# Fewer tiles in the second copy of x, a padded bias block, and a new written-out order

## The chip, the cores and the metric

The kernel runs on one core of a Trainium2 chip. The metric is the device time of one execution in microseconds (us), the median over runs. The engines are TensorE (PE), VectorE (DVE), ScalarE (ACT), GpSimd (POOL) and SyncE (SP), which here only issues transfers.

## The reference

Two branches over x (2048 rows, 512 columns), mixed by a gate:

```python
x = A_x
g = _sigmoid((x * gate_w).sum(-1, keepdims=True))
a = irfft2(rfft2(x) * (w_r + 1j * w_i))          # spectral branch, 2048 x 512
h = einsum("bsd,df->bsf", x, w1) + b1            # dense branch, 512 -> 1792 -> 512
b = einsum("bsf,fd->bsd", h * tanh(softplus(h)), w2)
return g * a + (1 - g) * b
```

Inputs and output are bfloat16.

## The kernel before

x is held as 16 tiles of 128 rows, tile t being the rows that are t modulo 16. The dense branch works in four chunks of four tiles. For each chunk c, 14 groups mm1_c_ft multiply w1 by the transposed x (xT) into PSUM; mish_c_ft on ACT adds b1 (b1f) and applies the activation; mm2_t_part multiplies by w2. In chunk 0 the first four groups are cut into halves by columns and by contraction (mm1a0_ft, mm1a1_ft, mm1b0_ft, mm1b1_ft).

The spectral branch: ts and td on DVE form sums and differences of x; s1 (PE), e2 (eviction), a10 and a11 (PE), eg (ACT), e1p and e1m (DVE) make the first transforms; r1w stores the result to a scratch in DRAM, r1r loads it turned round; s2 (PE), wm and wz (DVE, POOL), s2i (PE), e4, r2w and r2r do the same for the second axis; s1i, e5, a1i, gc, sap, sam, sbp, sbm go back. gdot, gpow, gcol and omg make the gate.

xT comes in two ways. Tiles 0 to 7 are transposed on PE (tr, L475) into PSUM and evicted (evx). Tiles 8 to 15 are loaded a second time in 16 small copies (ld_xq, rows of 256 bytes) into a buffer X4, which lies in the third part of act, and transposed from there in blocks by DVE (xt, L483). b1 is loaded by POOL's queue (ld_b1) as 14 rows into braw, transposed by PE (tr_small, L488) and evicted by DVE (ev_small, L490). At the start PE runs matmuls on constants (warm, L419) while nothing has been loaded.

The order is written out by hand. Every operation is a task with a number in the order in which the code adds it; the string ORDER lists the tasks by two digits in base 62, with a letter where a task may run on several engines and a digit for each PSUM bank. Each engine runs its own tasks in that order, and waits on semaphores for what a task reads, or overwrites:

```python
for t in order[ename]:
    ...
            eobj.wait_ge(sem_, val)
    ins = t.fn(eobj)
```

So a task that waits holds back everything behind it on its engine, loads included, as an engine's queue also issues its transfers. A task that writes a tile waits for the tile's last writer:

```python
for w in writes:
    _add(self.last_w.get(w))
    for rd in self.readers.get(w, ()):
        _add(rd)
```

Of the kernel before, what the change touches and what calls it, by code (L numbers as in the profile page):

```python
# [7 lines left out]
BF = mybir.dt.bfloat16  # L8
# [5 lines left out]
NT = 16  # L14
# [143 lines left out]
class _Graph:  # L158
# [89 lines left out]
DIGITS = "0123456789ABCDEFGHIJKLMNOPQRSTUVWXYZabcdefghijklmnopqrstuvwxyz"  # L248
ENGINE = {"p": "pe", "a": "act", "v": "dve", "g": "pool", "s": "sp"}
ORDER = (  # L250
    "000M1Wv02010P0Q0R0S0U1Xv0W0X0Y0Z04005060708090A0B0C0D0E0F0G0H0I0J0K0L030q0N0O1E70a1Fv0V0b0r1G30c0T111I61Hv0d6u"
    "70s1K0121Zv6z3701Jv1g41U61Yv1p11Lv0e1ia6v1hv1V71721rv745751qa1j40t731l1bv761av776w1s23A6x1k4791781u0f1t2131mv2"
    "051nv1wv1og0g0h0i6y0j7B31dv7A21a1vv7D11M72267C2302837F21cv7E1Nv242I529a26v7H71xv1ev2A325v7G2B12Ja2C7J01fv7I2K5"
    "2Q20u0v7L42u2M2L62Dv2Ra7N72Ev2a12v2Ov2S57M2w2Nv2T37K7P07O2Fg6p727g0k0l0m0n0o0p2x1y2U2ba2k56q142Vv2y6r1O2156s2l"
    "a2c12Pg2Wv2e2n52m32z1Pv6t2Xg2d67R42fv302gv1z2G2H0w2o0x7f12qv2hg2rg2Y162pv2Z2i2j2s1S7S2t17310y1A0z7g1018191R7Q3"
    "27h21Q3K1T7i33343536377j6387k393B3F3C7l07m1B3G3D3E3L7n77o7p17q7r07t47v77s7x37u7w7z08127y835848573H3I3J82808J18"
    "68K8L38N28P68M8O8R38S8T78Q8V23O33Wv3P53R8U8W1C3Q3Xv3S3T3Yg8X18Z23Zg3bv3U8Y3V8b78a8c8d18f33av3e8g3M8e7T73j33l3k"
    "13m3n3qv3cg8h53rv7U3o7W03N1D3uv3p3dg3vv8i7X3sg3y3f17Ya3tg3xg7Vv3ga4353wg4Av7Z77a3ha454Bv4Dg44046473z340a3i41a7"
    "c24Cg4849424I7d4Fv4Ev4Hg4Gg7bv4N54O34Vv4P4Q4R8j07ev877884Uv8A68B4S4Zv4T4Yv4c8k4J04Kv89a4Wg4Xg4La4bg4ag8D74d14f"
    "v8x58Cv8E4ea8Fv8z38y8G59129348H92957948Iv976908l08m8nv96989978o34M4g4h4i9A4l14mv4t25105974j52v4ua5H65Aa5P54n14"  # L260
    "o5X44v25305Iv5B74p4w4q5C4sg4rg4x8p4y5E5f64zg545gv5Qa5Ya5D50g565J15R59B2558qa5K9iv4k5n49C9D79jv5S5U5Fg5h25v65L5"
    "oa5M5wa9F35T9G5Gg5Z49H66336B55i9I64v57g5a58g9J19L05p36569lv9mv5Og5j5Wg5b5Vg9K9M6Ca5k5c9E8r15Ng9ov5x25y9pv6J46R"
    "0605lg5q5s6D75mg9k6Ka5eg6Sa5z5r5dg6661g8s8ta6E6F6Z46av9sv6h09rv62g5ug8u55tg679N29O6G8v8wa686Ag6L39n6T46U6W6M9P"
    "16O9uv6b29vv6c9Q69g9xv6ia6j06V9S69q9t6e6Hg9Ra6d6k9w6N6Ig9yv9T9V56fv9W6Xg6l6m6Yg9Z49z6gv9c26nv6Qg6Pg9Ua9X9YA0vA"
    "1v9f5A26ov9d9a9e9b9g9h"
)
NBF = 14
GD_N = 8
# [8 lines left out]
DENSE2 = {0: (0, 1), 1: (0, 1), 2: (0, 1, 2, 7), 3: (0, 1, 2, 7)}  # L277
LAST = ((0, 256), (256, 384), (384, 512))
NWARM = 16
NFILL = 2  # L280
PR = dict(tr=99.0, sp=95.0, mm1=88.0, mish=97.0, mm2=70.0, fin=98.0, gate=96.9, sum=98.5)


def _build(nc, A_x, A_w_r, A_w_i, B_x, B_w1, B_b1, B_w2, gate_w, out):
    cs = _build_consts()
    d_FM, d_GM, d_RT = (nc.inline_tensor(_bf16_bits(cs[n].reshape(128, -1)), name="c_" + n.lower()).bitcast(BF)
                                    for n in ("FM", "GM", "RT"))
# [3 lines left out]
    G = _Graph()  # L291
    es = ExitStack()
    with es:
        def sb(name, shape, dt):
            return es.enter_context(nc.sbuf_tensor(name, shape, dt))

        xo = sb("xo", [128, NT, 512], BF)
        xT = sb("xT", [128, 4, NT * 128], BF)
        Tg = sb("Tg", [128, 8192], BF)
        act = sb("act", [128, 3, NFT, 512], BF)  # L300
# [4 lines left out]
        rt = sb("rt", [128, 4096], BF)  # L305
# [2 lines left out]
        WT = sb("WT", [128, 2, 16, KR], BF)  # L308
        Abuf = sb("Abuf", [128, 8192], BF)
        Ybuf = sb("Ybuf", [128, 16 * 514], BF)  # L310
        braw = sb("braw", [14, 128], BF)
        b1f = sb("b1f", [128, NFT], F32)
        gdot = sb("gdot", [128, NT], F32)
        gcol = sb("gcol", [128, NT], F32)
# [1 line left out]
        ident = sb("ident", [128, 128], BF)  # L316
# [12 lines left out]
        REV = [31 - d for d in range(32)]  # L329
        REV0 = [(32 - d) % 32 for d in range(32)]  # L330
        XS = Abuf[:, 0:8192].rearrange("p (t r d) -> p t r d", t=NT, r=2)
        X4 = act[:, 2].rearrange("p f s -> p (f s)")[:, 0:4096].rearrange("p (t q d) -> p t q d", t=8, q=4)
        In2 = Abuf[:, 0:8192].rearrange("p (u g k) -> p u g k", u=8, g=4)
        T2r = Abuf[:, 0:8192].rearrange("p (b k) -> p b k", b=32)
        Yt = Ybuf[:].rearrange("p (t x) -> p t x", t=NT)
# [30 lines left out]
        def dma(name, dst, src, reads=(), writes=(), nbytes=0, deps=(), is_out=False, prio=None, queue="sp", bw=380e3, tail=1.1, nd=128, issue=0.62):  # L366
            t = G.add(name, queue, issue if issue != 0.62 or queue != "pool" else 1.0, lambda e: e.dma_start(dst, src),
                      reads=reads, writes=writes, lat=tail, deps=deps, prio=prio)
# [12 lines left out]
        def mm(n):
            return n / 2400.0 + 0.0025
# [10 lines left out]
        def pe(name, dur, fn, **kw):  # L393
            return G.add(name, "pe", dur, fn, lat=0.17, **kw)
# [7 lines left out]
        def tt(name, o, i0, i1, op, n, rate=1.0, engs=("dve",), lock=True, **kw):  # L402
# [8 lines left out]
              reads=["ones"], writes=["ident"])  # L411
# [3 lines left out]
        pw = _Ps([6])  # L415
        tw = []
        for i in range(NWARM + NFILL):
            n = 256 if i < NWARM else 128
            tw.append(pe(f"warm{i}", mm(n), lambda e, n=n: e.matmul(ps[:, pw.bank, 0:n], nc.const_aps.tensor(1.0, [128, 128], BF), nc.const_aps.tensor(1.0, [128, n], BF), start=True, stop=True),  # L419
                         alloc=pw if i == 0 else None, frees=[pw], prio=0.0, deps=tw[-1:]))  # L420

# [39 lines left out]
        dma("ld_ri", rt[:, 2048:4096], d_RT[:, 2048:4096], writes=["RI"], nbytes=128 * 4096, bw=300e3)
        WALL = [("W", i, j) for i in range(2) for j in range(9)]


        for t0, h in ((0, 0), (0, 1), (2, 0), (2, 1), (4, None), (6, None)):
            pt = _Ps(SPEC[::-1])
            hs = (0, 1) if h is None else (h,)
            c0, nc_ = 2 * hs[0], 2 * len(hs)

            def f_tr(e, t0=t0, c0=c0, nc_=nc_, pt=pt):  # L470
                ins = None
                for i in range(2):
                    for c in range(c0, c0 + nc_):
                        o = ((c - c0) * 2 + i) * 128
                        ins = e.transpose(psb[:, pt.bank, o:o + 128], xo[:, t0 + i, c::4], ident[:, :])  # L475
                return ins

            pe(f"tr{t0}" + ("" if h is None else "ab"[h]), 2 * nc_ * mm(128), f_tr, reads=[("x", t0 + i) for i in range(2)] + ["ident"], writes=[("ptr", t0, h)], alloc=pt)
            evict(f"evx{t0}" + ("" if h is None else "ab"[h]), 256 * nc_, lambda t0=t0, c0=c0, nc_=nc_: xT[:, c0:c0 + nc_, 128 * t0:128 * (t0 + 2)],
                  lambda pt=pt, nc_=nc_: psb[:, pt.bank, 0:256 * nc_].rearrange("p (c j) -> p c j", c=nc_), rate=2.0,  # L480
                  reads=[("ptr", t0, h)], writes=[("xT", t0 + i, q) for i in range(2) for q in hs], frees=[pt], engs=("dve",) if h is None else ("dve", "act"))
        for t0 in range(8, NT, 2):
            G.add(f"xt_{t0}", "dve", dve_dur(1024), lambda e, t0=t0: e.transpose(  # L483
                out=xT[:, :, 128 * t0:128 * (t0 + 2)], in_=X4[:, t0 - 8:t0 - 6, :, :].rearrange("p t q (d b) -> p b (t q) d", b=4)),
                reads=[("X4", a, q) for a in range(4) for q in range(4)] + [("act", 2, f) for f in range(t0 - 8, t0 - 6)],
                writes=[("xT", t0 + i, q) for i in range(2) for q in range(2)], lock=True, prio=PR["tr"] - 12.0 - 0.5 * t0)
        pb = _Ps(SPEC[::-1])
        pe("tr_small", 0.1, lambda e, pb=pb: e.transpose(psb[:, pb.bank, 0:14], braw[0:14, :], ident[0:14, 0:14]),  # L488
           reads=["braw", "ident"], writes=["ptb"], alloc=pb)
        G.add("ev_small", "dve", 0.2, lambda e, pb=pb: e.tensor_copy(out=b1f[:, :], in_=psb[:, pb.bank, 0:14]),  # L490
              reads=["ptb", "b1t"], writes=["b1f"], frees=[pb])
# [9 lines left out]
        for t in range(NT):  # L501
            if t % 2 == 0:
                p1 = _Ps(S1B)

                def f_s1(e, t=t, p1=p1):
                    ins = None
                    for i in range(2):
                        for q in range(4):
# [4 lines left out]
                                   writes=[("p1", t)], alloc=p1, prio=PR["sp"] + 0.4))  # L513
# [418 lines left out]
```

## Time and profile before

| | us |
|---|---|
| median of 3 runs | 129.48 (128.7 to 129.66) |
| the profiled execution | 129.57 |
| its span, first to last instruction | 127.8 |
| PE busy | 121.1 (95%) |
| DVE busy | 92.1 (72%) |
| ACT busy | 70.3 (55%) |
| POOL busy | 52.6 (41%) |

The profile is of one execution. The span is what its instructions cover; the rest of its time lies around it. A line such as L475 is a line of the kernel's code; helpers record several operations under one line (L403 is every tensor-tensor operation, L367 every transfer, L398 and L397 the evictions on ACT and DVE). Views used: the page's busy shares and its 40 slices of the span, the waits (who stood idle for whom), the timeline (start, duration, engine, line, what), the chain of waits that ended last, groups of instructions, and the transfers with their time from issue to landing.

### The profile page before, as it was taken

Reading aid. Unit: us, or ns where it says so; the run is one execution under the profiler, and the core shown is the slowest. Engines: PE = TensorE matmul, PEld = TensorE weight load, DVE = VectorE, ACT = ScalarE, POOL = GpSimd, SP = SyncE. Lnnn points to the kernel's source line nnn. Section 1 sums busy time; section 2 is a strip of 40 time slices with the busy share of each in tenths; the row PEclk is TensorE's granted clock in tenths of the full one; section 3 lists DMA queues with packets and bytes.
Section 4 is the critical chain, followed back from the end, with each engine's and each line's share of the span. In section 5 each row is a group of like instructions: output and inputs, shape, how many; then the busy total and the mean of one; then the engine's idle time right before and its main releaser. Section 6 shows DMA issues by size and latency. Waiting matters only on the chain.

```text
span 127.8 us, 2747 instructions
## 1 busy us (share of the span) xinstructions
PE 121.1 (95%) x1038; PEld 67.8 (53%) x1055; DVE 92.1 (72%) x190; ACT 70.3 (55%) x113; POOL 52.6 (41%) x82
## 2 busy tenths in 40 slices
PE   7799999999999969999999999999999999999992
PEld 5687666844444334444444444444576556454481
DVE  0769999999994089597679737020399999879853
ACT  4069999898839635416242235153299878354200
POOL 5000004110004457889685950000019979676500
DMA  3999999989878999800523008359200222022213
GB/s 85 352 395 388 286 175 177 206 235 266 255 186 224 258 374 371 341 24 5 164 63 109 0 0 229 107 146 405 105 0 5 82 85 82 0 87 82 82 42 122
DMA packets 23053, 21.10 MB, mean 165 GB/s; under 512 B 5888, under 2 KB 20096, under 8 KB 22912
## 3 DMA queue, kind: packets, MB, share of 16 engines
q1 hardware_dynamic: 22192, 20.13, 54.5%
q10 hardware_dynamic: 816, 0.79, 1.9%
q8 instruction: 8, 0.13, 0.5%
q14 instruction: 5, 0.04, 0.1%
q0 software_dynamic: 32, 0.00, 0.0%
HBM read 14.63 MB, written 6.29 MB: 164 GB/s over the span
## 4 chain that ended last, share of the span: by engine, by line
PE 79%; DMA 8%; DVE 5%; ACT 4%; issue 2%; SPq 0%; DVEq 0%
PE ps L797 36%; PE ps L767 30%; DMA Abuf<-scr 5%; DMA xo<-in_A_x_dram 3%; DVE Qb L739 3%; PE ps L534 2%; PE ps L509 2%; PE ps L717 2%; PE ps L689 2%; PE ps L638 2%; PE ps L728 2%; ACT Qb L733 1%; ACT act L782 1%; PE ps L475 1%; DVE xo L403 1%
## 5 line engine op out<-in xcount | busy, mean ns | idle before, releaser
L767 PE MATMUL ps<-xT,w_sb 128*128 128x512 bf16 (+1 forms) x230 | 52.0, 364 | 0.7 <-DVE cvec L645 0.2
L797 PE MATMUL ps<-w_sb,act 128*128 128x512 bf16 (+2 forms) x245 | 50.2, 355 | 0.7 <-issue 0.5
L782 ACT ACTIVATE act<-ps,b1f 128x512 bf16<-128x512 f32 x56 | 36.7, 689 | 24.2 <-PE ps L767 24.0
L797 PEld LDWEIGHTS ps<-w_sb,act 128*128 128x128 bf16 x252 | 23.0, 98 | 23.4 <-issue 0.6
L767 PEld LDWEIGHTS ps<-xT,w_sb 128*128 128x128 bf16 x240 | 22.2, 98 | 21.8 <-issue 0.8
L403 POOL TENSOR_TENSOR Tg<-Qb 128x256 bf16<-128x256 f32 x28 | 21.1, 785 | 23.6 <-DVE Qb L739 23.6
L403 POOL TENSOR_TENSOR Zb<-Qb 128x510 bf16<-128x510 f32 x16 | 19.9, 1267 | 3.6 <-DVE Qb L403 2.9
L403 DVE TENSOR_TENSOR Qb<-ps,WT 128x1024 f32<-128x1024 f32 x16 | 18.8, 1214 | 2.0 <-PE ps L638 2.0
L739 DVE SCALAR_TENSOR_TENSOR Qb<-ps,gcol,Qb 128x256 f32<-128x256 f32 x32 | 13.4, 472 | 1.6 <-PE ps L728 0.8
L550 POOL COPY Ybuf<-Ybuf 128x2 bf16<-128x2 bf16 x7 | 2.5, 361 | 24.0 <-DVE Ybuf L403 24.0
L750 DVE TENSOR_SCALAR xo<-ps,omg 128x512 bf16<-128x512 f32 x7 | 5.2, 745 | 9.4 <-PE ps L797 9.4
L563 DVE SCALAR_TENSOR_TENSOR Tg<-xo,Tg 128x512 bf16<-128x512 bf16 x16 | 10.9, 678 | 0.2
L403 DVE TENSOR_TENSOR Ybuf<-ps,Tg 128x512 bf16<-128x512 f32 x16 | 10.5, 683 | 0.5 <-PE ps L534 0.2
L398 ACT ACTIVATE Tg<-ps 128x1024 bf16<-128x1024 f32 (+1 forms) x8 | 7.4, 922 | 5.5 <-PE ps L509 5.3
L749 ACT ACTIVATE xo<-ps,omg 128x512 bf16<-128x512 f32 x7 | 4.8, 690 | 9.7 <-PE ps L797 9.7
L403 DVE TENSOR_TENSOR xo<-xo,Tg 128x512 bf16<-128x512 bf16 x14 | 9.9, 746 | 0.0
L398 ACT ACTIVATE Ybuf<-ps 128x1024 bf16<-128x1024 f32 x6 | 5.9, 1022 | 6.6 <-PE ps L689 6.6
L403 DVE TENSOR_TENSOR Abuf<-xo 128x1024 bf16<-128x1024 bf16 (+1 forms) x10 | 5.6, 578 | 4.8 <-DMA xo<-in_A_x_dram 4.8
L733 ACT ACTIVATE Qb<-ps,gcol 128x256 f32<-128x256 f32 x16 | 7.2, 474 | 1.2 <-PE ps L728 1.2
L568 POOL TENSOR_TENSOR gcol<-omg,gdot 128x16 f32<-128x16 f32 x1 | 2.9, 2943 | 11.2 <-DVE Tg L563 11.2
L398 ACT ACTIVATE Zb<-ps 128x512 bf16<-128x512 f32 x10 | 5.6, 597 | 1.3 <-PE ps L717 1.3
L397 DVE CAST Zb<-ps 128x512 bf16<-128x512 f32 x6 | 4.0, 685 | 1.9 <-PE ps L717 1.8
(59 smaller groups left out, 90.2 us busy)
## 6 DMA issues: line engine op xcount, KB each, us to landing
Abuf<-scr SPq DMA_DIRECT2D x8, 512.0 KB, 6.4
scr<-Ybuf SPq DMA_DIRECT2D x4, 512.0 KB, 3.3
w_sb<-in_B_w_dram SPq DMA_DIRECT2D x2, 896.0 KB, 9.9
out_dram<-xo SPq DMA_DIRECT2D x7, 256.0 KB, 2.0
xo<-in_A_x_dram SPq DMA_DIRECT2D x3, 512.0 KB, 7.0
scr<-Ybuf SPq DMA_DIRECT2D x6, 256.0 KB, 3.7
act<-in_A_x_dram SPq DMA_DIRECT2D x16, 64.0 KB, 5.9
rt<-c_rt SPq DMA_DIRECT2D x2, 512.0 KB, 8.0
```

The costliest lines, as they stand in the source:

```text
L397: fs = {"dve": ("dve", dve_dur(n, rate=rate), lambda e: e.tensor_copy(out=dst(), in_=src())), "act": ("act", act_dur(n), lambda e: e.activ ...
L398: "act": ("act", act_dur(n), lambda e: e.activation(dst(), src(), AF.Copy)),
L403: f = lambda e: e.tensor_tensor(out=o(), in0=i0(), in1=i1(), op=op)
L563: lambda e, t=t: e.scalar_tensor_tensor(out=junk, in0=xo[:, t, :], scalar=1.0, in1=gwb, op0=ALU.mult, op1=ALU.mult, accum_out=gdot[:, t:t ...
L568: G.add("gpow", "pool", 3.0, lambda e: e.tensor_tensor(out=gcol[:, :], in0=omg[:, :], in1=gdot[:, :], op=ALU.pow), reads=[("gd", t) for t ...
L733: lambda e, t=t, sl=sl, p5=p5: e.activation(gC[:, sl, :].rearrange("p (i n) -> p i n", i=2), ps[:, p5.bank, :].rearrange("p (i n) -> p i n ...
L739: lambda e, t=t, sl=sl, p5=p5, o=o, op=op: e.scalar_tensor_tensor(out=st1[:, sl, o::2, :], in0=ps[:, p5.bank, :].rearrange("p (i n) -> p i ...
L749: G.add_multi(f"bev_{t}", [("act", act_dur(512, True), lambda e: e.activation(xo[:, t, :], ps[:, pd.bank, :], AF.Copy, scale=omg[:, t:t + ...
L750: ("dve", dve_dur(512, True), lambda e: e.tensor_scalar(out=xo[:, t, :], in0=ps[:, pd.bank, :], scalar1=omg[:, t:t + 1], scalar2=None, op0 ...
L767: ins = e.matmul(ps[:, pd.bank, cols[0]:cols[1]], w1_sb[:, i, 128 * ft:128 * (ft + 1)], xT[:, i, 512 * c + cols[0]:512 * c + cols[1]], sta ...
L782: lambda e, ft=ft, pd=pd, hb=hb: e.activation(act[:, hb, ft, :], ps[:, pd.bank, :], AF.Mish, bias=b1f[:, ft:ft + 1]),
L797: ins = e.matmul(ps[:, pd.bank, cs_], act[:, hb, ft, 128 * tl:128 * (tl + 1)], w2_sb[:, ft, cs_], start=(ft == 0), stop=(ft == NFT - 1))
```

## The change

- The second copy X4 holds tiles 12 to 15 only: the 16 ld_xq copies are of 32 KB instead of 64 KB. Tiles 8 to 11 are transposed by PE: two new groups tr8 and tr10 (8 transposes each) with evictions evx8 and evx10 on DVE replace xt_8 and xt_10.
- braw has 128 rows; a DVE memset (bz) sets it to zero, ld_b1 fills the first 14 rows, tr_small transposes the whole block.
- Three idle matmuls of 256 columns follow the first 16 (warm16 to warm18), instead of two of 128.
- ORDER is new, and with it the PSUM banks and the engines of some evictions.

```diff
-NFILL = 2
+NFILL = 3
...
-        braw = sb("braw", [14, 128], BF)
+        braw = sb("braw", [128, 128], BF)
...
-        X4 = act[:, 2].rearrange("p f s -> p (f s)")[:, 0:4096].rearrange("p (t q d) -> p t q d", t=8, q=4)
+        X4 = act[:, 2].rearrange("p f s -> p (f s)")[:, 0:2048].rearrange("p (t q d) -> p t q d", t=4, q=4)
...
-            n = 256 if i < NWARM else 128
+            n = 256
...
-        dma("ld_b1", braw[:, :], B_b1.rearrange("(ft p) -> ft p", p=128), writes=["braw"], nbytes=3584, queue="pool")
+        G.add("bz", "dve", 0.2, lambda e: e.memset(braw[:, :], 0.0), writes=["braw"])
+        dma("ld_b1", braw[0:14, :], B_b1.rearrange("(ft p) -> ft p", p=128), writes=["braw"], nbytes=3584, queue="pool")
...
-                dma(f"ld_xq{a}{q}", X4[32 * a:32 * a + 32, :, q, :], xv[32 * q:32 * q + 32, 8:16, 128 * a:128 * a + 128],
-                    writes=[("X4", a, q)], nbytes=32 * 8 * 256, bw=165e3, nd=256, issue=0.5)
+                dma(f"ld_xq{a}{q}", X4[32 * a:32 * a + 32, :, q, :], xv[32 * q:32 * q + 32, 12:16, 128 * a:128 * a + 128],
+                    writes=[("X4", a, q)], nbytes=32 * 4 * 256, bw=160e3, nd=128, issue=0.5)
...
-        for t0, h in ((0, 0), (0, 1), (2, 0), (2, 1), (4, None), (6, None)):
+        for t0, h in ((0, 0), (0, 1), (2, 0), (2, 1), (4, None), (6, None), (8, None), (10, None)):
...
-        for t0 in range(8, NT, 2):
+        for t0 in range(12, NT, 2):
...
-        pe("tr_small", 0.1, lambda e, pb=pb: e.transpose(psb[:, pb.bank, 0:14], braw[0:14, :], ident[0:14, 0:14]),
+        pe("tr_small", mm(128), lambda e, pb=pb: e.transpose(psb[:, pb.bank, 0:128], braw[:, :], ident[:, :]),
```

The task numbers of ORDER, read against the order in which the code adds the tasks, give these beginnings of the engines' queues:

```
SP   before: ld_x0 ld_x2 ld_ms ld_fm ld_w1_4_0 ld_x4 ld_x8 ld_w1_8_0 ld_w1_8_1 ld_x12 ld_gm ld_xq00 ...
SP   after:  ld_xq30 ld_xq20 ld_xq10 ld_x0 ld_xq31 ld_x2 ld_xq21 ld_ms ld_fm ld_w1_4_0 ld_x4 ld_x8 ...
ACT  before: table ld_w1_0_0 ld_w1_0_1 ld_w1_4_1 e2_0b e2_2a mish_0_2 eg_0 mish_0_3 ...
ACT  after:  table ld_w1_0_0 ld_w1_0_1 evx0b evx2a e2_0b ld_w1_4_1 e2_2b mish_0_2 eg_0 eg_2 ...
DVE  before: ts0 td0 evx0a evx0b td2 evx2a ts2 evx2b e2_0a ev_small e2_2b td4 ts4 e1p_0 ...
DVE  after:  td0 bz ts0 evx0a ts2 evx2b td2 ev_small e2_0a e2_2a ts4 td4 e1p_0 ...
POOL before: ones ebz ident ld_b1 ...
POOL after:  ebz ones ident ld_b1 ...
PE   before: warm0-17 tr0a tr0b tr2a mm1a0_1 tr2b mm1a0_2 mm1a1_2 s1_0 tr_small s1_2 mm1a1_1 mm1b0_2
             mm1b1_2 mm1a0_3 mm1a1_3 a10_0 mm1b0_3 mm1b1_3 mm1b0_1 a10_2 mm1b1_1 a11_0 mm1_0_4 ...
PE   after:  warm0-15 tr0a warm16-18 tr0b mm1a0_2 mm1a0_3 tr2a tr2b s1_0 mm1a1_3 mm1a1_2 tr_small mm1b0_3
             s1_2 mm1a0_1 mm1b0_2 mm1b1_2 mm1a1_1 mm1b0_1 a10_0 a11_0 mm1b1_3 a10_2 mm1_0_4 ...
```

Later on PE: tr8 and tr10 stand behind mm1_0_13, one mm1 group fewer stands ahead of s2_0 (six of chunk 2 instead of seven), and s1i_0 follows mm2_8_1 instead of mm2_9_0. On SP, all loads of the filter (ld_W) stand ahead of most of the stores r1w, and of the stores r1w14a and r1w14b only ld_rf is left between them and r1r0; before, seven loads were. On both sides 57 transfers stand ahead of r1r0.

More of the change, by code (lines that the diff above doesn't have):

```diff
@@ L250 @@
 ORDER = (
[L251 to L265, printed above, removed]
+    "0o0k02030g0N000430p0506071bv08090A0B0C0W0D0E0F0G0H0I0J011G20Q0l0R0S0K0L0T0V0Y0M1av0Z0a0b1Hv0O1I67310P7840X1cv1"
@@ new lines @@
+    "K01Ja1M51Nv1dv1La1k213790c741ma1Y71Z7A1lv1t51uv0U0h6y00q1ev1fv0s75766z701n31o70m1va0d0e777B1w21p7D61y7C7E1O524"
+    "1711x31qv1rv7F47H70i721Pv2C51hv25a0t1gv7G7I2M17J01zv20v2Dv0r0n21v2631jv0f2742Na7L7282Av2U229v1Q67K0u2E01iv3E7N"
+    "57M2Va1Rv2G2O72F32P47P12Bg2Iv2Hv7O1sv2Q2Sv7Q2Rv2e57R72W32o12X40v0w0x2Jg2y2fa2g62z2pa0y7T0147V52Y300z1S21U12av1"
+    "011122Zv2bg7U157W2h3222Tg6t531320j232K6u7S6v2q72i2kv2jv2s7j07k2r416176w181Tv6x2tv192lv1A1B2L2uv2vv2c2d2m2n2w2x"
+    "331Vv34351W1C363O3P3J3K3L7l77n3371D1E7m3Q7p53R7r77t27o1F7q7s7v57x67z07u7y3M7w388113N3982801X8323A8485486871897"
@@ new lines @@
+    "883B3C3D3F8N38O8P28R08T58Q8S8U8V18A8X03S43bv3U3av3dg3T63ev3G8W3cg3fv8Y3V3W8Z23X3Y8b08c8d38a8e8f58h48g8j38k3n63"
+    "p3hg3o13q3uv3r3s3gg3vv3Z8l53H3I3i7X03zv8m8i3yv7Y7Za7a37b3j44713ka3wg7d0493t423la3xg4Fv40g7e7ca4864Ev41g4317g54"
+    "A4B4Iv7fa44a4Gg7h45a4Jv4Hg3m4R14Zv4C4Kg4S64D7ia4T4M4U4V4W4Yv4Lg8n44bg4X8B38C8o8E58Da4N04Oa4Pa4cv4ag4dv4eg8F4g8"
+    "H68Gv4fg4h24ja9174iv929319509748I94969908K79A469B2988L4Q4k4l8Ja9C9D28p48q8Ma9E4m4n4p74x15565D24ya56a8rv5Ev8s34"
+    "qa4z15L75051524r04s4t54g5F64u5Ma5G5T45b55I5725ca53g5Uv8t585H4vg5j75ka8ua5A9F05V55W595N44wg4o5O9H69I9G5Kg5Y5r19"
@@ L266 @@
+    "nv5d75e5P8v35Q5Bg5z467660a68a9mv5Cg5sv6F09J25Jg5X5g9pv5l56Ga9K9qv5Zg616625ag5f645Rg8w6915Sg5m5n9L79tv5o5hg9o9r"
+    "5t4636N09sv8xa5u5w9M5v9N25ig9O6Oa5pg9P39u6V76d28y56A6Wa5qg6ev6H76X49Q6B9vv6Y9wv6I5xg9R29S6P366g6C65g6l66J5yg6E"
+    "g6Q6K6S6ma6f08z9zv9yv6Z6R6Dg9x6Lg6a9T6A06g90a6h6n76Mg6o6i9U9W39X9Z09a9d2A1vA2v6Ug6Tg6p9Vv6qA36kv6bg9YaA4v6jv6s"
+    "v6cgA5vA69b6rg9g69c9e9f9h9i9j49k9l"
 )
@@ L457, in _build @@
             dma(f"ld_Wz{i}", WT[1:32:2, i, 0, :], Vm[:, 63, :], writes=[("W", i, 8)], nbytes=16 * 514, bw=110e3, nd=16)
-        dma("ld_rf", rt[:, 0:2048], d_RT[:, 0:2048], writes=["RF"], nbytes=128 * 4096, bw=300e3)
+        dma("ld_rf", rt[:, 0:2048], d_RT[:, 0:2048], writes=["RF"], nbytes=128 * 4096, bw=170e3)
         for h in range(2):
@@ L481, in _build @@
                   reads=[("ptr", t0, h)], writes=[("xT", t0 + i, q) for i in range(2) for q in hs], frees=[pt], engs=("dve",) if h is None else ("dve", "act"))
-        for t0 in range(8, NT, 2):
+        for t0 in range(12, NT, 2):
             G.add(f"xt_{t0}", "dve", dve_dur(1024), lambda e, t0=t0: e.transpose(
-                out=xT[:, :, 128 * t0:128 * (t0 + 2)], in_=X4[:, t0 - 8:t0 - 6, :, :].rearrange("p t q (d b) -> p b (t q) d", b=4)),
-                reads=[("X4", a, q) for a in range(4) for q in range(4)] + [("act", 2, f) for f in range(t0 - 8, t0 - 6)],
+                out=xT[:, :, 128 * t0:128 * (t0 + 2)], in_=X4[:, t0 - 12:t0 - 10, :, :].rearrange("p t q (d b) -> p b (t q) d", b=4)),
+                reads=[("X4", a, q) for a in range(4) for q in range(4)] + [("act", 2, f) for f in range(t0 - 12, t0 - 10)],
                 writes=[("xT", t0 + i, q) for i in range(2) for q in range(2)], lock=True, prio=PR["tr"] - 12.0 - 0.5 * t0)
         pb = _Ps(SPEC[::-1])
-        pe("tr_small", 0.1, lambda e, pb=pb: e.transpose(psb[:, pb.bank, 0:14], braw[0:14, :], ident[0:14, 0:14]),
+        pe("tr_small", mm(128), lambda e, pb=pb: e.transpose(psb[:, pb.bank, 0:128], braw[:, :], ident[:, :]),
            reads=["braw", "ident"], writes=["ptb"], alloc=pb)
```

## The prediction

> **What bounds the kernel now.** I read the page's busy rows first, then the waits of TensorE (PE), then the start and the one hole in PE's timeline.
>
> ```profile
> span 127.8 us, 2747 instructions
> PE 121.1 (95%) x1038; PEld 67.8 (53%) x1055; DVE 92.1 (72%) x190; ACT 70.3 (55%) x113; POOL 52.6 (41%) x82
> PE   7799999999999969999999999999999999999992
> ...
> PE ps L638 <- DMA Abuf<-scr: 1.0, 1, 1.0
> PE ps L419 <- PEq L917: 0.8, 1, 0.8
> PE ps L475 <- DMA xo<-in_A_x_dram: 0.8, 1, 0.8
> PE ps L797 <- issue: 0.5, 3, 0.2
> PE ps L717 <- DVE Qb L739: 0.2, 1, 0.2
> PE ps L767 <- DVE cvec L645: 0.2, 1, 0.2
> PE ps L767 <- issue: 0.2, 1, 0.2
> ```
>
> PE is busy 95% of the span, and all its waits together are 3.7 us, of which 0.8 is the wait for the program's start and 0.8 the wait for the second block of x. From then on it has about 2.1 us of waiting, of which 1.04 is one hole in front of s2_0. So PE's own queue sets the end: whatever holds PE up near the start reaches the end, unless it is taken out of that hole; and an operation added to PE costs its length.
>
> The rows of the start, from the timeline:
>
> ```profile
> 0.80 0.86 SPq L367 DMA_DIRECT2D xo<-in_A_x_dram  x2
> 1.07 1.50 ACTq L367 DMA_DIRECT2D w_sb<-in_B_w_dram  x3
> 1.47 0.78 POOL L367 DMA_DIRECT2D braw<-in_B_b_dram  x1
> 3.15 1.16 SPq L367 DMA_DIRECT2D xo<-in_A_x_dram  x2
> 4.05 0.76 DVE L403 TENSOR_TENSOR Abuf<-xo 128x512 bf16<-128x512 bf16 x2 [4.05 <-DMA xo<-in_A_x_dram]
> 4.07 0.63 PE L475 MATMUL ps<-ident,xo 128*128 128x128 bf16 x8
> 5.49 0.41 PE L475 MATMUL ps<-ident,xo 128*128 128x128 bf16 x4 [0.78 <-DMA xo<-in_A_x_dram]
> 7.36 0.18 PE L488 MATMUL ps<-ident,braw 14*128 14x14 bf16 x1
> 10.78 0.81 PE L767 MATMUL ps<-xT,w_sb 128*128 128x512 bf16 x3
> ```
>
> The reader is to see four moments. ld_x0 is issued at 0.80 and lands at 4.05, 3.25 us later; PE's first transposes start then. ld_x2 is issued behind it (1.24) and lands at 5.49. The transpose of b1 (tr_small) runs at 7.36 without a wait, since its load was issued at 1.47. The first whole group of 512 columns, mm1_0_4, runs at 10.78.
>
> **The change, part by part: the start.** Three xq copies now stand ahead of ld_x0 on SP. Five issues fill 0.80 to 3.15, 0.47 us each, so ld_x0 is issued at 0.80 + 1.41 = 2.21 and, by the same 3.25, lands at 5.46. From both sides: the six xq issues of the row below take 0.51 each, which gives 5.6; on the low side, the two halves of w1 on ACT's queue get the engines first and are further along when x0 begins.
>
> ```profile
> 20.15 3.07 SPq L367 DMA_DIRECT2D act<-in_A_x_dram  x6
> ...
> 2.00:3.00 1.00, 1.00 (x7) 0.69 (x6) 0.00 (x0) 0.28 (x2) 0.38 (x2) 1.00 0.79 219
> 3.00:4.00 1.00, 1.00 (x8) 0.77 (x7) 0.00 (x0) 0.00 (x0) 0.00 (x0) 1.00 0.80 245
> 4.00:5.00 1.00, 0.70 (x12) 0.54 (x9) 0.95 (x3) 0.00 (x0) 0.00 (x0) 1.00 1.05 389
> ```
>
> x0's 256 KB at 389 GB/s instead of 245 (last column) would come 0.4 earlier, 5.05. I take 5.3, the middle; PE's start moves by 1.25. PE has nothing that covers it: the warm-up matmuls end at 4.06.
>
> Then the load of b1. The new memset bz writes braw on DVE, and ld_b1 writes the same tile, so POOL's ld_b1 waits for bz. bz stands on DVE behind td0, and td0 waits for x0. So a load that was issued at 1.47 is now issued after x0 has landed: 5.3, td0 0.38 (two in 0.76), bz 0.2 (the nearest row is POOL's memset of a 128x128 tile), 5.9. What it takes from there:
>
> ```profile
> 0.79 0.20 POOL L408 MEMSET ident<- 128x128 bf16 x1 [0.29 <-POOLq L917]
> ...
> DMA to landing us min/median/max: 5.3/5.3/5.3
> ...
> out_dram<-xo SPq DMA_DIRECT2D x2, 32.0 KB, 1.5
> ```
>
> The view of the tile braw has 5.3 us from the issue to the landing of 3.5 KB. It is the only load on POOL's queue, and I take it: 5.9 + 5.3 = 11.2. Low bound: POOL's 0.78 plus the 1.5 of the quickest small transfer of SP, 2.3, which gives 8.2. The Trainium skill ("DMA: Bandwidth & Descriptors", section "Anatomy of one DMA — SWDGE (gpsimd) path") puts a load from GpSimd at about 2.0 us plus its bytes at 436 GB/s; by that rule b1 would be there at 7.9 and the wait below would be none. The trace's 5.3 differs from it, and the measurement decides.
>
> When does PE get to tr_small? x0 5.3; tr0a, three warm-up matmuls of 256 columns (0.11 each) and tr0b, 0.8 us: 6.1. evx0a on DVE comes after td0, bz and ts0 (5.3 + 0.38 + 0.2 + 0.38 = 6.26) and takes 0.42: 6.7; two mm1 halves of 0.22: 7.15. ld_x2 is now sixth on SP, issued at 3.15, and by its old 4.24 lands at 7.4; tr2a, tr2b, s1_0 and two more halves: 0.45 + 0.45 + 0.43, 8.7. There PE waits for b1 until 11.2, some 2.5 us; ev_small, behind it on DVE, holds e2_0a and e2_2a back, and on ACT every mish waits for b1f.
>
> The shift: tr_small starts at 11.2 instead of 7.36, 3.84 later, with one half matmul (0.22) more already done: +3.6.
>
> ```profile
> 8.09 1.09 PE ps L767 x10
> ...
> 13.98 0.45 PE ps L475 x8
> ```
>
> (Ten halves in 1.09; eight transposes in 0.45, from the chain.) The padded tr_small is at most one more such transpose, 0.06: left out. Next late is ld_w1_4_1, which now stands on ACT behind evx0b, evx2a and e2_0b: e2_0b can start at 8.2 and ends at 8.8.
>
> ```profile
> w_sb<-in_B_w_dram ACTq DMA_DIRECT2D x3, 256.0 KB, 5.0
> ...
> xo<-in_A_x_dram SPq DMA_DIRECT2D x2, 256.0 KB, 3.7
> ```
>
> By the 5.0 of its queue it lands at 13.8 (by 3.7, 12.5). PE needs it for mm1_0_4, which stands 2.6 us of work behind tr_small (six halves, s1_2, three a1 groups): 13.85 by the sum above. So it is covered, by the wait for b1; without that wait it would be the one that holds PE, from 11.35 to between 12.5 and 13.8.
>
> **The transposes.** tr8 and tr10 add 16 transposes to PE: 2 x 0.45, 0.89 by the finer 0.0557 each, with nothing to hide in. On DVE two transposes are replaced by two evictions:
>
> ```profile
> L483 DVE STREAM_TRANSPOSE xT<-act 128x1024 bf16<-128x1024 bf16 x4 | 4.8, 1226 | 0.0
> L397 DVE COPY xT<-ps 128x1024 bf16<-128x1024 bf16 x2 | 1.4, 688 | 0.0
> ```
>
> That frees 1.1 us of DVE, but mm1_2_0, which reads them, stands 14 groups of four 512-column matmuls later on PE; worth nothing. If evx10 came after those 14 groups, PE would wait for it, at its whole lateness.
>
> **The hole before s2_0.** It is set by the queue of SP:
>
> ```profile
> 30.88 3.79 SPq L367 DMA_DIRECT2D scr<-Ybuf  x5
> ...
> 37.93 1.27 SPq L367 DMA_DIRECT2D WT<-in_A_w_i_dram  x2
> 39.59 0.35 SPq L367 DMA_DIRECT2D Abuf<-scr  x1
> ...
> 45.88 0.63 PE L638 MATMUL ps<-Abuf,rt 64*32 64x256 bf16 x32 [1.04 <-DMA Abuf<-scr]
> ...
> scr<-Ybuf SPq DMA_DIRECT2D x4, 128.0 KB, 2.5
> ```
>
> r1r0 is issued at 39.59, behind 57 others, and lands 6.25 later. After the change 57 still stand ahead of it, but the last stores r1w14 are now 55th and 56th instead of seven loads earlier. At the old pace the 56th is issued at 37.9, lands 2.5 later, and r1r0 goes at 40.4: data at 46.7. Half-size xq copies may make the queue 1 to 2 us faster; a late DVE could hold it, but the five stores above were issued from 30.9, so their data was ready, and 3.6 later is still before 37.9. PE came to s2_0 at 44.84; it now has one matmul group less in front (0.86), the shift and the transposes: 44.84 - 0.86 + 3.6 + 0.89 = 48.5. It no longer waits: -1.04.
>
> **The rest.** About ten evictions of the later stages change between DVE and ACT, and s1i_0 is one mm2 half group (1.5 us) nearer to s2i_3, 13.6 us of matmuls behind it instead of 15.1.
>
> ```profile
> 76.35 0.57 PE ps L689 x32
> ...
> 83.20 1.76 SPq L367 DMA_DIRECT2D Abuf<-scr  x4
> ...
> DMA to landing us min/median/max: 4.0/5.3/6.6
> ```
>
> s2i_3 ended at 76.9, so s1i_0 would come at 90.5; r2r0, issued at 83.2, lands in 4.0 to 6.6 us, by 89.8 at the latest, so there is cover. PE waits for only about 1 us in that whole part, so I count zero, with 0 to -0.8 and up to +0.8 as bounds.
>
> **Sum**, against the profiled execution (129.57 us: the span of 127.8 and 1.8 around it, which stay; the median of the runs is 129.48, the same for this purpose): +3.6 (start) + 0.89 (transposes) - 1.04 (hole) = +3.45, 133.0 us.
>
> **Rivals.**
>
> Quick b1. POOL's load takes 2.3 us instead of 5.3 (for: 3.5 KB should not need 5; against: the only row). Then ld_w1_4_1 decides: mm1_0_4 at 12.5 to 13.8 instead of 10.78, with one half not yet done, +1.9 to +3.2; plus 0.89 less 1.04; and by the r1r0 estimate PE then waits at most 0.1. Time 131.3 to 132.6.
>
> Cold clock. PE stands still some 2.5 us before tr_small, after a first stretch in which it is half idle. The matmuls of 256 columns at the start are slow: about five new ones in the microsecond from 2 to 3 (the row above counts seven with those that overlap its edges), where the later ones take 0.109. If the wait brings the slow speed back for some 2.6 us, half of it is lost, +1.3, and up to +1.8 with a second such stretch: 134.3 to 134.8. Against it: the 0.78 us hole at 4.7 left the speed as it was. The Trainium skill ("TensorE: Matmul & The Clock Gate", section "Part 1: The HAM clock gate") has the slow clock return after an idle window of about 3.4 us; by that rule 2.5 us is too short unless b1 comes a microsecond later still.
>
> Not slower: the start costs almost nothing. x0's landing is set by the slow first microseconds of the transfers (219 and 245 GB/s) and not by its issue, so it lands by 4.4, and b1 takes 2.3. PE is at tr_small near 7.8 and at mm1_0_4 near 10.5, w1_4_1 (issued at 7.9, 3.7) lands at 11.6; shift +1.0, and 0.89 - 1.04 on top, and part of the other 1 us of PE's waits taken away by the new evictions: 129.4 to 130.4. It decides only if x0 lands before 4.4 and b1 within 3 us of its issue, both. Speaks for it: half a megabyte of 256-byte rows less in the queue. Against: five issues in a row at 0.47.
>
> **How the numbers follow.** Sum as worked out (132.4 to 133.8): 0.55. Quick b1: 0.20. Cold clock: 0.12. Not slower: 0.09. Something in the later stages that I count as zero going wrong by more than 2 us: 0.04. Predicted 133.0, range 130.7 to 134.8. A measurement of this kernel tells about 1% from no change, 128.2 to 130.8: faster 0.03 (only if all waits of PE vanish too), same 0.08, slower 0.89.
>
> **What would show it.** In the profile after: DVE's first instruction at 5.0 to 5.6 instead of 4.05; POOL's DMA issue near 5.9 instead of 1.47; PE waiting 2 to 3 us for the DMA of braw ahead of the L488 transpose, which starts near 11; mm1_0_4 near 13.9; no wait at the first L638, near 48.5; 16 more L475 matmuls. Wrong if the L488 row has no wait in front of it, if the transpose starts before 9, or if PE's matmuls of 256 columns are 0.2 us apart after it.

## The result and the profile after

The changed kernel takes 137.53 us (median of 4 runs, 137.43 to 137.97) against 129.16 before in the same comparison: ratio 1.065, interval 1.060 to 1.071. It is slower, as forecast, but by 8.4 us and not by 3.5. The page of the profile after, first the busy rows and the slices of the span (PEclk is the granted clock of PE in tenths), then PE's waits:

```profile
span 136.2 us, 2791 instructions
PE 125.9 (92%) x1055; PEld 71.3 (52%) x1072; DVE 87.5 (64%) x185; ACT 75.3 (55%) x121; POOL 53.4 (39%) x80
PE   7591959999999999999999999999999999999993
PEclk9999599999999999999999999999999999999999
...
PE ps L489 <- DMA braw<-in_B_b_dram: 3.0, 1, 3.0
PE ps L768 <- ACT act L783: 1.5, 2, 1.4
PE ps L476 <- DMA xo<-in_A_x_dram: 1.5, 1, 1.5
```

All the loss is in the first six of the 40 slices; from there on PE is as full as before. (Line numbers are one higher than before, so L489 is tr_small, L476 the transposes, L510 s1, L768 mm1, L783 mish; in most variants below they are five higher again: L494, L481, L515, L773, and L424 the idle matmuls.) Rows picked from the timeline of the start, and s2_0:

```profile
2.18 0.43 SPq L367 DMA_DIRECT2D xo<-in_A_x_dram  x1
5.92 0.43 DVE L403 TENSOR_TENSOR Abuf<-xo 128x512 bf16<-128x512 bf16 x1 [5.92 <-DMA xo<-in_A_x_dram]
6.72 0.78 POOL L367 DMA_DIRECT2D braw<-in_B_b_dram  x1 [5.33 <-DVE Abuf L403]
10.22 0.37 ACTq L367 DMA_DIRECT2D w_sb<-in_B_w_dram  x1
13.65 0.29 PE L489 MATMUL ps<-ident,braw 128*128 128x128 bf16 x1 [2.99 <-DMA braw<-in_B_b_dram]
19.51 0.81 PE L768 MATMUL ps<-xT,w_sb 128*128 128x512 bf16 x3 [1.39 <-ACT act L783]
53.74 0.63 PE L639 MATMUL ps<-Abuf,rt 64*32 64x256 bf16 x32
```

The steps that the prediction named are there one by one: x0 lands at 5.92, ld_b1 is issued behind bz at 6.72, PE waits for it before tr_small, and there is no wait ahead of s2_0 (L639). What PE loses: tr_small comes at 13.65 instead of 7.36, 6.3 later; mm1_0_4 at 19.5 instead of 10.78, 8.7 later; s2_0, with one matmul group less in front of it, at 53.7 instead of 45.88, 7.9 later.

One row must not be believed as it stands. The wait of 1.39 at mm1_0_4 is put down to ACT. But mm1_0_4 reads nothing that mish writes, and its bank was not held by a mish. The row also has three of the group's four matmuls: the record of the first is missing (in the profile before too), and the weights of the group were loaded from 19.26 on, before that mish ended at 19.33:

```profile
18.65 0.68 ACT L783 ACTIVATE act<-ps,b1f 128x512 bf16<-128x512 f32 x1
19.26 0.56 PEld L768 LDWEIGHTS ps<-xT,w_sb 128*128 128x128 bf16 x4 [1.32 <-issue]
```

So mm1_0_4 began near 19.3, and PE waited some 1.2 us for it, from 18.1. The load that it does need, ld_w1_4_1, was issued on ACT at 10.22; the view of its landing, for the stretch in which it is the only issue of that tile:

```profile
L367 ACTq DMA_DIRECT2D w_sb<-in_B_w_dram x1: 374/374/374, 10.2 to 10.2; - x1
...
DMA to landing us min/median/max: 8.9/8.9/8.9
```

10.22 + 8.9 = 19.1: that load is what mm1_0_4 waited for. The experiments e1 and e6 below bear this out.

Then the clock, by stretches of one microsecond (length, PE busy, granted clock, share of the transfer engines, GB/s):

```profile
12.00:13.00 1.00, 0.00 (x0) 1.00 1.08 412
13.00:14.00 1.00, 0.35 (x3) 0.78 1.05 402
14.00:15.00 1.00, 1.00 (x10) 0.50 1.11 282
15.00:16.00 1.00, 1.00 (x8) 0.50 1.07 196
16.00:17.00 1.00, 1.00 (x7) 0.52 1.14 261
17.00:18.00 1.00, 1.00 (x16) 1.00 1.33 251
```

At the end of the wait for b1 the granted clock falls to half and stays there for 3.4 us (13.56 to 16.97 in the trace's records of the clock). The work between tr_small and mm1_0_4 took 4.5 us (13.65 to 18.1). In e4 and e7 below, which have the same order there and no slow clock, it takes 2.7 (7.49 to 10.19 and 10.80 to 13.51), so the slow clock cost 1.8.

There is an earlier slow stretch that this column does not show. The first record of the clock in this trace is of 10.14; for the time before it the view prints 1.00, but the rows are those of half speed:

```profile
8.27 1.06 PE L476 MATMUL ps<-ident,xo 128*128 128x128 bf16 x8
9.12 1.06 PE L510 MATMUL ps<-FMs,Abuf 128*128 128x128 bf16 x8
```

From the start of one row to the next, eight transposes take 0.85 us here; in the chain of before they took 0.45. From x0's landing PE needs 4.7 us to reach the wait for b1 (5.94 to 10.67); in e7, at full speed, 2.8 (8.03 to 10.80). On PE the wait for b1 covers this. But ld_w1_4_1 stands on ACT behind evictions of that work: it was issued 4.3 us after x0's landing, in e6, at full speed, 3.15 (3.93 to 7.08). What this 1.15 cost at mm1_0_4 was not tested.

### The profile page after: what moved, and what is told of

Same layout as the page of the kernel before. It is cut to its first block, busy times and chain, and to the rows that moved or that the text cites. A ratio compares the mean times of both kernels' runs of the same rounds, so it can differ in the third digit from the quotient of the medians.

```text
span 136.2 us, 2791 instructions
## 1 busy us (share of the span) xinstructions
PE 125.9 (92%) x1055; PEld 71.3 (52%) x1072; DVE 87.5 (64%) x185; ACT 75.3 (55%) x121; POOL 53.4 (39%) x80
## 4 chain that ended last, share of the span: by engine, by line
PE 86%; DMA 8%; ACT 1%; issue 1%; SPq 1%; DVE 1%
PE ps L768 36%; PE ps L798 35%; DMA braw<-in_B_b_dram 5%; DMA xo<-in_A_x_dram 3%; PE ps L729 3%; PE ps L535 3%; PE ps L718 3%; PE ps L510 3%; PE ps L690 2%; PE ps L639 1%; PE ps L476 1%; ACT act L783 1%; SPq L367 1%; DVE Abuf L403 1%; ACT Tg L542 0%
## 5 line engine op out<-in xcount | busy, mean ns | idle before, releaser
L768 PE MATMUL ps<-xT,w_sb 128*128 128x512 bf16 (+1 forms) x231 | 53.4, 374 | 2.0 <-ACT act L783 1.5
L783 ACT ACTIVATE act<-ps,b1f 128x512 bf16<-128x512 f32 x56 | 36.7, 687 | 15.1 <-PE ps L768 14.9
L768 PEld LDWEIGHTS ps<-xT,w_sb 128*128 128x128 bf16 x240 | 23.0, 102 | 22.9 <-issue 2.2
L403 POOL TENSOR_TENSOR Tg<-Qb 128x256 bf16<-128x256 f32 x29 | 22.2, 801 | 22.0 <-DVE Qb L740 22.0
L750 ACT ACTIVATE xo<-ps,omg 128x512 bf16<-128x512 f32 x11 | 7.6, 689 | 11.3 <-PE ps L798 11.3
L751 DVE TENSOR_SCALAR xo<-ps,omg 128x512 bf16<-128x512 f32 x3 | 2.2, 745 | 15.4 <-PE ps L798 15.4
L551 POOL COPY Ybuf<-Ybuf 128x2 bf16<-128x2 bf16 x4 | 0.7, 192 | 26.3 <-DVE Ybuf L403 26.3
L403 DVE TENSOR_TENSOR xo<-xo,Tg 128x512 bf16<-128x512 bf16 x14 | 10.8, 796 | 0.0
L398 ACT ACTIVATE Tg<-ps 128x1024 bf16<-128x1024 f32 (+1 forms) x7 | 6.3, 898 | 5.6 <-PE ps L510 5.5
L398 ACT ACTIVATE Zb<-ps 128x512 bf16<-128x512 f32 x12 | 6.8, 597 | 4.3 <-PE ps L718 3.8
L476 PE MATMUL ps<-ident,xo 128*128 128x128 bf16 x48 | 4.6, 249 | 1.5 <-DMA xo<-in_A_x_dram 1.5
L397 DVE COPY xT<-ps 128x1024 bf16<-128x1024 bf16 (+1 forms) x6 | 3.6, 596 | 3.3 <-PE ps L476 3.3
```

Of the source, the lines that this page charges most:

```text
L398: "act": ("act", act_dur(n), lambda e: e.activation(dst(), src(), AF.Copy)),
L403: f = lambda e: e.tensor_tensor(out=o(), in0=i0(), in1=i1(), op=op)
L750: G.add_multi(f"bev_{t}", [("act", act_dur(512, True), lambda e: e.activation(xo[:, t, :], ps[:, pd.bank, :], AF.Copy, scale=omg[:, t:t + ...
L768: ins = e.matmul(ps[:, pd.bank, cols[0]:cols[1]], w1_sb[:, i, 128 * ft:128 * (ft + 1)], xT[:, i, 512 * c + cols[0]:512 * c + cols[1]], sta ...
L783: lambda e, ft=ft, pd=pd, hb=hb: e.activation(act[:, hb, ft, :], ps[:, pd.bank, :], AF.Mish, bias=b1f[:, ft:ft + 1]),
```

## The experiments

Two theories stood at first. Theory 1: three loads that come late at the start, x0, b1 and ld_w1_4_1, cover one another in part, and the slow clock is added. The rival: the transposes and the new order of the later stages cost a part of it. All variants move tasks within their engine's queue after ORDER has been read, and nothing else, unless said:

```diff
+        for eng, name, before in (...):
+            o = order[eng]
+            t = next(t for t in o if t.name == name)
+            o.remove(t)
+            o.insert(next(i for i, u in enumerate(o) if u.name == before), t)
         self.order = order
```

**e1_bz_first**: `("dve", "bz", "td0")`, so the memset comes first and b1 is loaded at 1.5 again.

> The changed kernel with the memset bz first on DVE, ahead of td0, so that ld_b1 is issued near 1.5 instead of 6.72. Theory 1 (two late loads stand one behind the other: b1, and ld_w1_4_1, which is issued at 10.2 behind e2_0b on ACT and landed 8.9 us later): the 3.0 us wait before tr_small goes, but PE then waits at mm1_0_4 until about 19, so the time stays at 137.5, within 0.7. Rival (the wait for b1 and the slow clock after it are the loss): 137.5 - 3.0 - 1.25 = 133.3.

Measured: 139.0 us, ratio 1.075 (1.069 to 1.082) to before. The wait for b1 is gone, and nothing is won. Its waits of PE:

```profile
PE ps L773 <- DMA w_sb<-in_B_w_dram: 4.2, 1, 4.2
PE ps L481 <- DMA xo<-in_A_x_dram: 2.2, 1, 2.2
```

PE now stands 4.2 us at mm1_0_4, and here the profile names the load itself. The four matmuls begin at 18.0, 1.3 earlier than in the changed kernel, but the clock fell to half again at 17.72, for 3.4 us:

```profile
18.00 1.86 PE L773 MATMUL ps<-xT,w_sb 128*128 128x512 bf16 x4 [4.17 <-DMA w_sb<-in_B_w_dram]
```

So taking away the wait for b1, the largest one in the list of the changed kernel, wins nothing by itself: the load behind it lands only 1.3 earlier, and the longer wait for it brings back the slow clock.

**e2_w1_early**: `("act", "ld_w1_4_1", "evx0b")`, third on ACT's queue as before.

> The changed kernel with ld_w1_4_1 third on ACT's queue, ahead of evx0b, as before the change. Theory 1: only the 1.4 us wait at mm1_0_4 goes, since PE has stood waiting for b1 until 13.65 and has run slowly to 17: 136.1. Rival (the late w1 is what holds everything, as b1 is covered by it): 133 or less.

Measured: 136.01 us, ratio 1.052 (1.044 to 1.060). The number is the one expected, but not by the way expected:

```profile
8.07 0.61 PE L481 MATMUL ps<-ident,xo 128*128 128x128 bf16 x4 [3.67 <-DMA xo<-in_A_x_dram]
14.56 0.23 PE L494 MATMUL ps<-ident,braw 128*128 128x128 bf16 x1 [1.74 <-DMA braw<-in_B_b_dram]
```

With a third 256 KB load ahead of it on ACT's queue, x0 lands at 8.05 instead of 5.92, though it is issued at the same time; tr_small comes 0.9 later still. Here too the printed clock of 1.00 is not to be believed at the start: the first record is of 12.33, and the eight transposes before it take 0.86.

```profile
10.40 1.06 PE L481 MATMUL ps<-ident,xo 128*128 128x128 bf16 x8
11.26 1.06 PE L515 MATMUL ps<-FMs,Abuf 128*128 128x128 bf16 x8
```

But behind tr_small no slow stretch follows. So of what w1 gave (1.2) x0 took 0.9, and the rest of the gain is the slow stretch that did not come (1.8). In the profiled executions these make 2.1, and 2.0 was measured (135.97 against 137.97).

**e3_bz_w1**: both moves.

> Both: bz first on DVE and ld_w1_4_1 third on ACT. Theory 1: both waits and the slow clock go: 137.5 - 3.0 - 1.4 - 1.25 = 131.9. Rival (the extra transposes and the new order of the later stages cost several us): above 133.5.

Measured: 133.37 us, ratio 1.033 (1.028 to 1.037). One wait is left, for x0, which lands at 7.7; the slow clock follows it:

```profile
PE ps L481 <- DMA xo<-in_A_x_dram: 3.3, 1, 3.3
...
8.00:10.00 2.00, 2.00 (x16) 0.51 1.05 332
10.00:12.00 2.00, 2.00 (x22) 0.63 0.97 335
```

**e4_bz_w1_x**: both, and the five xq copies from the head of SP's queue moved ahead of ld_Wp10, that is behind ld_x12.

> As e3_bz_w1, and the five xq copies at the head of SP's queue moved behind ld_x12, so that ld_x0 is the first transfer again. Theory 1: x0 lands at 4.05 instead of 5.92, 1.9 less than e3: 130.0, what is left over the kernel before being the 0.89 of the transposes less the hole before s2_0. Rival (x0's place is covered by something else): as e3, 131.9.

Measured: 128.93 us, ratio 0.997 (0.995 to 1.000): the time of the kernel before. Its PE waits:

```profile
PE ps L424 <- PEq L923: 0.8, 1, 0.8
PE ps L515 <- DMA FMs<-c_fm: 0.2, 1, 0.2
```

The whole change apart from three places in the queues (the new transposes, the padded block, the order of the later stages) costs nothing together. The rival falls. And x0's place is worth 4.4 us here (133.37 to 128.93), far more than its 1.4 us of later issue: 3.6 of it is the landing (7.72 in e3, 4.08 here), most of the rest the slow stretch behind it in e3.

```profile
4.08 0.76 DVE L408 TENSOR_TENSOR Abuf<-xo 128x512 bf16<-128x512 bf16 x2 [3.09 <-DMA xo<-in_A_x_dram]
```

The next three take e4 and put back one late load at a time, or fill a wait.

**e5_b1_late**: e4 without the move of bz.

> e4_bz_w1_x with the memset bz behind td0 again: only b1 is late. Theory 1: x0 lands at 4.1, ld_b1 is issued near 4.8 and lands 5.3 to 6.9 later, 10.1 to 11.7; PE is at tr_small at 7.5 and waits 2.6 to 4.2: 128.9 + 2.6 to 4.2 = 131.5 to 133.1, plus up to 1.2 for the slow clock. Rival (b1 alone is absorbed later): 129 to 130.

Measured: 131.65 us, ratio 1.025 (1.019 to 1.031), 2.7 above e4. Three of the four executions took 131.5 to 131.8 at a mean clock of 1.0, one 133.18 at 0.987. In the profile, one of the three, PE's only new wait is the one for b1, and its load took the same 5.3 as before the change:

```profile
10.13 0.23 PE L494 MATMUL ps<-ident,braw 128*128 128x128 bf16 x1 [2.40 <-DMA braw<-in_B_b_dram]
...
L372 POOL DMA_DIRECT2D braw<-in_B_b_dram x1: 780/780/780, 4.8 to 4.8; - x1
...
DMA to landing us min/median/max: 5.3/5.3/5.3
```

**e6_w1_late**: e4 without the move of ld_w1_4_1.

> e4_bz_w1_x with ld_w1_4_1 behind evx0b, evx2a and e2_0b again: only that load is late. Theory 1: it is issued near 7.6 and lands 5.0 to 8.9 later, 12.6 to 16.5; PE is at mm1_0_4 at 10.2: 128.9 + 2.4 to 6.3 = 131.3 to 135.2. Rival (its long landing came from the late b1 and the small copies in front): lands 3.7 later, 11.3, 130.0.

Measured: 135.58 us, ratio 1.051 (1.047 to 1.056), 6.7 above e4 and above the range expected: the wait of 4.25 us is within it, the clock was not counted.

```profile
14.43 1.86 PE L773 MATMUL ps<-xT,w_sb 128*128 128x512 bf16 x4 [4.25 <-DMA w_sb<-in_B_w_dram]
...
14.00:16.00 2.00, 1.57 (x4) 0.56 1.10 222
16.00:18.00 2.00, 2.00 (x20) 0.58 1.15 246
```

The single costs are 4.4 (x0), 2.7 (b1) and 6.7 (w1), 13.8 together; all three at once cost 8.6 (137.53 less 128.93). They cover one another.

**e7_fill**: e3, with 27 more idle matmuls behind the first 16 (the last of them is done 28 times, 43 in all).

```diff
-lambda e, n=n: e.matmul(...)
+lambda e, n=n, i=i: [e.matmul(...) for _ in range(28 if i == 15 else 1)][-1]
```

> e3_bz_w1 with 28 more idle matmuls of 256 columns behind the first 16, which fill PE's wait for x0 (4.4 to 7.7) up to about 7.1. Theory: the slow clock from 8 to 11.5 comes from that idle stretch, so it stays at full speed, and half of 3.4 us is won less what is covered: 133.4 - 1.2 to 1.7 = 131.7 to 132.2, with a granted clock of 1.0 throughout. Rival (the clock has nothing to do with it, or PE waits in that stretch anyway): 133.4.

Measured: 132.48 us, ratio 1.029 (1.025 to 1.032), 0.9 below e3; direction and clock as expected, the size below the range. x0 landed 0.16 later than in e3 (7.88) and the idle matmuls held PE until 8.03, so a part of the difference is hidden by that.

```profile
0.83 7.36 PE L424 MATMUL ps<-const-bfloat16-1.0 128*128 128x256 bf16 x43 [0.83 <-PEq L923]
...
8.00:10.00 2.00, 1.94 (x27) 1.00 1.01 352
10.00:12.00 2.00, 2.00 (x30) 1.00 1.01 394
```

Matmuls whose results nobody reads shorten the kernel: without them the same stretch ran at a clock of 0.51 and 0.63. The slow clock comes from the idle stretch.

**e8_tiny_first**: e4, with ld_Wz0, ld_Wz1 and ld_ms moved ahead of ld_x0, so that its issue is late but no xq copy stands in front.

> e4_bz_w1_x with three other small transfers (two of 8 KB and one of 32 KB) ahead of ld_x0 on SP instead of the xq copies, so that it is issued at the same 2.2. Theory H1 (x0 loses its place to the 768 KB of w1 on ACT's queue, whatever stands in front): x0 lands at 7 or later, 132.5 to 133.5. H2 (the 256-byte rows of the xq copies slow it): it lands at 2.2 + 3.25 = 5.5, 130.3.

Measured: 132.75 us, ratio 1.033 (1.026 to 1.039). The three issues took longer than the xq copies', so x0 was issued at 2.75:

```profile
2.75 0.91 SPq L372 DMA_DIRECT2D xo<-in_A_x_dram  x2
...
6.94 0.42 PE L481 MATMUL ps<-ident,xo 128*128 128x128 bf16 x4 [2.54 <-DMA xo<-in_A_x_dram]
```

It landed 4.2 us after its issue: more than the 3.3 of e4, where it is first, and less than the 5.5 of e3 (2.18 to 7.72), where the xq copies and the same three w1 loads are in flight. So neither theory alone: losing the first place costs about 0.9 beyond the issue, and with the xq copies about 1.3 more (one profile each; e2 and e7 have 5.9 and 5.7 in e3's place). That the w1 loads take their part is seen with the xq copies in front alike: with two w1 loads on ACT's queue x0 landed at 5.92 (after) and 6.48 (e1), with three at 7.72 (e3), 7.88 (e7) and 8.05 (e2). How the engines share among the queues is left open.

**e9_tr_twice**: e4 with the 16 new transposes done twice.

```diff
-                for i in range(2):
+                for i in (0, 1) * (2 if t0 >= 8 else 1):
```

> e4_bz_w1_x with the eight transposes each of tr8 and tr10 done twice, 0.89 us more of work on PE. e4 has no wait ahead of s2_0 to take it, so theory 1: 128.9 + 0.9 = 129.8. Rival (transposes on PE hide somewhere): 128.9.

Measured: 129.80 us against 128.93 of e4, both steady within 0.6: 0.87 us for 16 transposes, near their price of 0.89. By the ratios of e9 and e4 to before, 1.005 and 0.997, it is 1.0.

**e10_warm_first**: e4 with warm16 to warm18 ahead of tr0a.

> e4_bz_w1_x with the three idle matmuls warm16 to warm18 moved ahead of tr0a. They take 0.32 us of PE between tr0a and tr0b once x0 is there. Theory: up to 0.3 is won, 128.6. Rival (the eviction that follows, or the load of the tables that s1_0 waited 0.2 us for, decides there; or they now delay tr0a): 128.9 or a little more.

Measured: 129.17 us, ratio 1.000 (0.997 to 1.003): nothing won. x0 was there before the idle matmuls ended, and they delayed the first transposes to 4.84, against 4.20 in e4.

**e11_before_s2**: the kernel before, with mm1_2_7 ahead of s2_0.

> The kernel before the change with mm1_2_7 moved ahead of s2_0 on PE, so that 0.86 us of work fills the 1.04 us hole. Theory (PE's queue is what sets the end): 129.3 - 0.86 = 128.4. Rival (the chain behind s2_0 over DVE and POOL sets the later stages): 129.3.

Measured: 128.70 us, ratio 0.998 (0.996 to 1.001). The hole is gone from PE's waits and the profiled span is 126.9, but the comparison does not tell the time from the kernel before: not settled.

**e12_before_tr_twice**: the kernel before with tr4 and tr6 done twice, as in e9 with `t0 in (4, 6)`.

> The kernel before the change with the transposes of tr4 and tr6 done twice: 16 more on PE, 0.89 us, all of them ahead of the hole. Theory (the hole takes them): PE comes to s2_0 0.89 later and waits 0.15 instead of 1.04, so 129.3. Rival (their length is added): 130.2.

Measured: 130.14 us, ratio 1.006 (1.002 to 1.011), between the two, with runs from 129.3 to 132.0. In its profile the wait ahead of s2_0 is gone, so the hole did take them there; but the second block of x came 0.6 us later in this execution than in the one shown of before (6.10 instead of 5.49), and that moves PE by as much. The landing at the start differs from run to run by about as much as this experiment was to show, so it decides nothing.

No version beats the kernel before beyond doubt: e4 and e11 are level with it or a few tenths of a per cent below.

## Why the prediction was right in its direction and wrong in its size

- PE's queue sets the end, and a delay at its start goes through: right. 8.7 us at mm1_0_4, 8.4 at the end.
- x0's landing was taken at 5.3, by the old 3.25 us from issue to landing or less; it was 5.92, 3.74 after its issue. The low bound, that the w1 loads would be out of the way sooner, had the sign wrong: they were in the way, and a third one put x0 2.1 later (e2).
- b1 behind bz, bz behind td0, td0 behind x0: right, link by link. The load was taken at 5.3 us from its one row; it took 6.9 here (5.3 in e5, 4.4 in e1, 3.4 in e8). So tr_small came at 13.65 instead of 11.2. The rival of a quick b1 falls: no run has 2.3. The rule that the prediction weighed beside it, about 2.0 us for such a load (the Trainium skill, "DMA: Bandwidth & Descriptors", section "Anatomy of one DMA — SWDGE (gpsimd) path"), differs from every one of these rows.
- ld_w1_4_1: this is the step furthest off. It was seen, and put at 5.0 us from its issue at 8.8, so at 13.8, to be covered by the wait for b1 with nothing to spare. It was issued at 10.2 and took 8.9, so it landed at 19.1. The 5.0 was the median of three loads, issued when ACT's queue had two others and SP's had sent little; at 10.2 SP's queue was deep in x8, w1_8, x12 and the xq copies. Which of these made it slow was not tested. By e1 that load alone would have held PE to 18.0, whatever b1 did.
- The slow clock, which the sum put at nothing, came, as a rival with 0.12 had it: 3.4 us at half speed, 1.8 us lost, the upper end of the rival's price. The prediction's own sign of being wrong is there: ten matmuls of 256 columns took 2.06 us behind tr_small (15.01 to 17.07), 0.2 apart. It should have had a greater chance, as the forecast itself left PE 2.5 us idle. And the sum priced the work behind x0 at full speed, though it had read that the first matmuls are slow: with x0 late, PE stayed at half speed until 10.14, and ld_w1_4_1 was issued 4.3 us after x0's landing instead of 3.5. The page named there (the Trainium skill, "TensorE: Matmul & The Clock Gate", section "Part 1: The HAM clock gate") lets the half clock follow an idle window of about 3.4 us and says that the window is free-running. The runs agree in the length of the slow stretch and in the free running (last section); as to what starts it they differ: idle stretches of 2.2 us (e1), 2.5 (e8) and 3.0, all shorter than the window, were followed by it, one of 2.4 (e5) was not.
- The stretch from tr_small to mm1_0_4 was counted as six halves and priced at 2.6 us. It has seven (each is two matmuls of 256 columns, 0.22 together), and the price holds: 2.7 in e4 and e7.
- The transposes: 0.89 forecast, 0.87 by e9. The hole before s2_0: gone, as forecast, and the later stages nothing, as counted, with e4 as the proof of both together.

The miss in one line: mm1_0_4 came at 19.3 instead of 13.85, since tr_small was 2.45 later than forecast, the slow clock took 1.8 and the late w1 1.2. Of these 5.4 us, 0.4 came back further on, and the median (137.53) lies 0.4 below the profiled execution (137.97). So the mechanism of the start was right, and the terms that failed are the two landings, b1's (5.3 put, 6.9 measured) and w1's (5.0 put, 8.9 measured), and the full-speed clock. The range left them out because the upper side of each landing was taken from rows of the first microseconds, before most of the loads were issued, and the clock stood only in a rival.

## What to carry to other kernels

A small operation inserted ahead of a load's issue (here a memset on another engine) can tie that load to the arrival of other data; follow the wait through the queues before its own cost is counted. The time from issue to landing belongs to the moment and not to the transfer alone (256 KB took 3.3 to 8.9 us here): bound it by rows from a stretch with as many bytes in flight. And the longest wait in a list may be covered by the next one: take it away in an experiment before it is blamed. Where a clock column has no record yet, read the speed from the distance of equal matmuls.

## What the runs showed of the hardware that was not expected

- The same 256 KB of x0 landed 3.3 us after their issue at the head of SP's queue (e4), and 3.7 (after), 4.3 (e1), 5.5 (e3) and 5.9 (e2) with three issues ahead of them; these three cost the kernel 3.8 (e8) to 4.4 us (e3), where x0's issue moved by 2.0 and 1.4.
- The granted clock fell to 0.5 for about 3.4 us after PE had stood still for as little as 2.2 us, and filling such a stretch with matmuls on constants was worth 0.9 us (e7).
- In each profile the recorded changes of the clock at the start lie whole multiples of 3.41 us apart, at a phase that differs from run to run (after: 10.14, 13.56, 16.97; e6: 4.02, 14.26, 17.67). Windows of that grid at full speed in which PE stood still for 2.15 us or more in all (e8 2.15, e1 2.2, after 2.9, e3 3.1) were followed by half speed, one with 1.7 (e2) was not. The idle stretch of e5, 2.4 us, was cut by the grid into 1.0 and 1.4, and passed.
- 3.5 KB on POOL's queue took 3.4 to 6.9 us from issue to landing.
